# Fixed issue order from a table in place of ranks, in a packed-attention and gated-FFN kernel on one core

## The chip, the cores and the metric

The kernel runs on one core of a Trainium2 chip, in one launch. The metric is the device time of that launch in microseconds. Five instruction streams matter here: PE (matmuls and transposes), DVE, ACT, POOL and SP, which issues nearly all DMA transfers. Each stream runs in the order in which the program was written; an instruction that waits holds everything behind it on its own stream.

## What is computed

```python
def sm_attn(qq, kk, vv):                       # scale = 1/8
    a = softmax(scale * qq @ kk.T); return a @ vv
p_packed = sm_attn(p, k, v)                    # 32 queries per head over 576 rows
out      = sm_attn(q, p_packed, p_packed)      # 576 queries over 32 rows
x = out with the 8 heads side by side          # (8, 576, 512)
h = relu(x @ w_in)                             # (8, 576, 1024)
conv_out = 3-tap convolution of h along the sequence, per channel, with conv_w
return (h * sigmoid(conv_out)) @ w_out         # (8, 576, 512)
```

Batch 8, 8 heads, sequence 576, head dimension 64, float32 in and out.

## The kernel before, in words

The work is cut into streams, written as Python generators; each `yield Step(...)` says on which engine the next few instructions stand, what they wait for and which buffers they take and give back. There are 16 groups `g` of four heads (two groups a batch). For each group there is a stream for the loads of k, q (`load_kq`) and v (`load_v`), for the queries (`queries`: pm, pT), for the transposes of k and q (`head_transpose`: kT, qT; on PE and ACT for g < 4, one DVE transposition for g >= 4) and one for both attentions (`attention`: first scores from kT and pT, `nm`, exp into `a`, its transposes `a1T`, the product with v, `pb`, `ppT`, second scores from qT and ppT, softmax on DVE in tile `s`, transposed into `a2t`, split into `a2hi` on ACT and `a2lo` on DVE).

Weights come in eight transfers of 1 MB (`load_weight`), are decoded on ACT and DVE (tile `tmp`, L283 to L289) and put together on PE (`weight`, L341). For each batch `packed_weight` multiplies ppT into w_in, in two halves (`ghi`, `glo`). `ffn1(b, j)` makes one of 8 blocks of 128 channels of batch b: 12 matmuls (L649), relu into `hbuf` (L660), convolution on ACT and DVE (L664 to L670), sigmoid (L674), product (L676). `ffn2(m)` makes one of 36 tiles of 128 output rows: the split into `xhi` (ACT, L692) and `xlo` (DVE, L695), 24 matmuls into bank `fo` (L711), a copy into `o` (ACT, L716) and the output transfer (SP, L718).

Buffers bound how far streams run ahead: three `kq` slots for k and q of g >= 2, two slots for v, three PSUM tiles `big`, two for `s`, `x` and `o`. PE runs spare matmuls (`idle`, L259) where the planner saw a hole, up to the first output tile.

`Flow` is a planner that runs while the program is written. It holds a clock for each engine and for the transfers (`data`), and estimates for every step when it could start. `Flow.run` takes the engine that can go on first, and among the steps of that engine that are ready the one with the lowest rank in the table RANKS. So the ranks, with the costs in `Step`, set the order on every engine, and the SP queue's too. No estimate is left in the program that runs: only the order, and where the spare matmuls stand.

Of the kernel before, what the change touches and what calls it, by code (L numbers as in the profile page):

```python
# [20 lines left out]
RANKS = dict(  # L21
    k=[-411.0614, -56.32, -268.848, -369.0188, -10.607, 1.2892, 3.3386, 133.9183, 102.8098, 879.0292, 1255.3289, -152.1904, 3265.748, 2301.2373, 4073.7935, 5527.8193],
    v=[610.8614, 749.1152, 765.1742, 986.139, 1329.6858, 1269.6691, 1710.2848, 2149.7283, 1487.6843, 2549.2198, 5360.8956, 3717.5078, 5649.9351, 6699.0695, 6718.2568, 5821.5235],
    q=[153.3881, 2678.8613, -36.5409, -534.5143, 15.659, 555.9669, 1381.0816, 1482.4838, 1796.3623, 2083.4696, 3164.823, 3316.2358, 2551.7338, 5842.8484, 5523.9367, 5847.3967],
    queries=[5129.5747, -76.4517, 1831.777, 5486.9661, 2287.2198, 3228.3676, -560.937, 3911.8645, 5818.0089, 1224.2293, 2191.3475, 6075.1066, 4118.8338, 957.2377, -307.2209, 3615.5839],
    kT=[5736.7974, -483.8463, 553.7556, 408.255, 3083.2521, 5765.4763, 3896.7744, 5207.2595, 5358.4206, 3202.632, 5269.8891, 5371.5274, 5299.2063, 120.4482, 1271.3159, 2568.6227],
    qT=[1822.3814, 149.2968, 1218.3584, -269.2693, 1711.232, 1654.8561, 2171.3878, 3701.8394, 5672.096, 353.4709, 4066.7032, 5429.4678, 2268.9292, 5358.7206, 222.3705, 2101.3936],
    attention=[551.6318, 5443.0779, 4911.4625, 3277.6066, 65.8326, -4.185, 2216.4119, 775.0971, 3.0273, -63.566, 3554.4746, 194.6953, -141.7721, 2717.9598, 5675.3416, 2685.8275],
    sums=[2212.5273, 6593.67, 2120.4894, 2288.466, 2267.3881, 3298.9219, 539.0862, 5551.4175, 278.5043, 4140.9774, 2298.0652, 5441.9071, 5447.2342, 5340.7613, 2224.1344, 2195.0737],
    first=[3485.5317, 5992.9594],  # L30
    p=[-602.8021, 423.7176, 2583.1976, 2679.7272],
    load=[539.5951, 5201.6034, 3915.0356, -142.7698, -520.5537, 6101.7696, 3.6438, 3085.3699],
    weight=[3894.055, 415.5091, 5692.3927, 1094.9361, 2353.1416, 3840.1368, 5430.0718, 5676.1554],
    packed=[3577.1581, 5645.4193, 6697.6272, 2233.1226, 823.9014, 5464.0982, 4050.5266, 1240.3014, 1363.631, -311.5196, 5146.9566, 223.8075, 1458.215, 3320.7258, -22.7754, 5405.3068],
    ffn1=[382.8943, -307.4377, 670.6109, 3512.0211, 3061.8509, -696.3821, 708.7212, -523.2062, 2230.3122, 778.609, 3794.9833, 1385.1523, 171.9222, 5875.7606, 5891.3708, -268.9693, -27.916, 229.1412, 6086.4179, 3961.4117, 1253.6236, -298.9416, -92.0749, 506.8444, 1021.7865, 2235.1843, 1822.6814, 1818.6582, 289.8734, -373.3513, 123.6805, 971.6445, -505.8058, 2261.7916, 2059.7915, 2244.506, 2287.2636, 3251.6386, 4026.9332, 3882.595, 5829.3173, 1396.2015, 3883.7763, 6025.1134, -420.7776, 1005.7303, 426.1176, 4453.7934, 4265.8601, 1304.3038, 25.1843, -325.5138, 2534.8185, 47.5927, 5893.1673, 5388.9951, 5605.6557, 107.7366, 46.4049, 2226.8256, 5622.8384, 5211.2071, -79.5994, 387.443],
    ffn2=[3213.9683, 5587.2785, -45.6475, 2059.3311, 5970.2991, -826.7935, 1356.9098, 2161.583, -208.5721, 5444.3776, 960.4174, 2239.558, 966.066, 1050.7084, 5488.7732, 3774.109, 1199.7934, 5443.758, 5765.0603, 2151.9103, 5849.4642, 5597.3931, 4837.0348, -88.4009, 3979.5915, 2137.3678, 245.2455, 3761.219, 176.6706, 5898.133, 5524.2367, 204.1131, 1753.915, 261.0496, 165.4131, 5407.7056],
    hold=-10.7483,
# [14 lines left out]
class Flow:  # L52
# [32 lines left out]
    def add(self, rank, stream):
        step = next(stream, None)
        if step is not None:
            self.streams.append([rank, stream, step, (0.0, None)])

    def earliest(self, step, last):  # L90
        froms = [last]
        for event in step.after:
            if event not in self.done:
                return None
            froms.append(self.done[event])
        for name in set(step.take):
            n = step.take.count(name)
            if len(self.tokens[name]) < n:
                return None
            froms.append(self.tokens[name][n - 1])  # L100
# [49 lines left out]
    def run(self):  # L150
        while self.streams:
            ready = []
            for s in self.streams:
                at = self.earliest(s[2], s[3])
                if at is not None:
                    ready.append((at, s))
            assert ready, "no stream can go on"
# [1 line left out]
            engine = first[2].engine
            pick = None  # L160
            for at, s in ready:
                step = s[2]
                if step.engine != engine or at > now:
                    continue
# [1 line left out]
                if pick is None or rank < pick[0]:
                    pick = (rank, s)
            s = pick[1]
            step = s[2]
            at = now  # L170
# [23 lines left out]
            following = next(s[1], None)  # L194
            if following is None:
                self.streams.remove(s)
            else:
                s[2], s[3] = following, end
# [3 lines left out]
def tile_packed_attention_conv_gate(  # L202
# [517 lines left out]
    def add(kind, i, stream):  # L720
        flow.add(RANKS[kind][i], stream)

    for g in range(NGT):
        add("k", g, load_kq(g, "k", k))
        add("v", g, load_v(g))
        add("q", g, load_kq(g, "q", q))
        add("queries", g, queries(g))
        add("kT", g, head_transpose(g, "k"))
        add("qT", g, head_transpose(g, "q"))
        add("attention", g, attention(g))  # L730
        add("sums", g, sums(g))
    add("first", 0, conv_weight())
    add("first", 1, identities())
# [43 lines left out]
```

## Time and profile before

| | |
|---|---|
| time, median of three runs | 429.14 us (428.72 to 429.59) |
| the profiled execution: its own time, its span | 428.88 us, 426.9 us |
| PE busy, DVE busy, ACT busy in the span | 410.5 us (96%), 342.4 us (80%), 322.1 us (75%) |
| transfers | 47.2 MB, mean 111 GB/s over the span |

Span is from the first to the last instruction of the execution; the time has 1.98 us more around it. Matmuls are pipelined and their ends are modelled, so a busy PE is one that has work, not one at its peak. The busy share is a mean over stages: up to about 60 us the transfers move 218 to 357 GB/s in nearly every slice of the page, later 2 to 185.

### The profile page before, as it was taken

The page shows a single profiled execution, that of the slowest core. Times are in us where ns is not written, and L with a number is a line of the kernel's source. Part 1 is how long each engine was busy: PE and PEld are TensorE (multiplying, and loading weights), DVE is VectorE, ACT ScalarE, POOL GpSimd, SP SyncE. Part 2 cuts the span into 40 slices and gives each one's busy share as a digit, 9 for nine tenths or more (in the row PEclk, how much of TensorE's full clock was granted, in tenths as well). Part 3 has the DMA queues.
Part 4 walks back from the last instruction along what each step waited for, and adds up shares of the span by engine and source line. Part 5 has one row for each costly group of instructions (what it writes and reads, how often), then busy time and mean ns, then how long its engine had stood idle before and what let it go on. Part 6 is the DMA issues. An engine that isn't in the chain of part 4 may idle for free.

```text
span 426.9 us, 8189 instructions
## 1 busy us (share of the span) xinstructions
PE 410.5 (96%) x3347; PEld 325.6 (76%) x3347; DVE 342.4 (80%) x488; ACT 322.1 (75%) x509; POOL 1.6 (0%) x13
## 2 busy tenths in 40 slices
PE   4899989999999999999999999999999999999996
PEld 3665667777977797788778978877788888887885
DVE  0388889999998999999999798899889964865220
ACT  3697979999976978798876787889779865763221
POOL 1000000000000000000000000000000000000000
PEclk9999999999999999999999999999999999999999
DMA  8999998069478791782588039080110001000111
GB/s 298 357 272 345 218 254 140 2 85 175 77 141 166 97 185 44 150 122 81 83 150 122 26 95 146 2 137 26 40 36 26 25 25 51 25 26 25 51 49 49
DMA packets 135620, 47.21 MB, mean 111 GB/s; under 512 B 119700, under 2 KB 127892, under 8 KB 135584
## 3 DMA queue, kind: packets, MB, share of 16 engines
q1 hardware_dynamic: 135552, 46.67, 50.1%
q8 instruction: 26, 0.43, 0.5%
q14 instruction: 10, 0.08, 0.1%
q0 software_dynamic: 32, 0.02, 0.0%
HBM read 37.25 MB, written 9.44 MB: 109 GB/s over the span
## 4 chain that ended last, share of the span: by engine, by line
PE 83%; ACT 8%; DMA 5%; SPq 2%; DVE 1%; issue 1%; DVEq 0%; ACTq 0%
PE fo L711 42%; PE big L649 22%; PE sm L711 4%; PE big L460 3%; PE big L597 3%; PE sm L523 2%; PE big L514 2%; SPq L421 2%; DMA q<-in_q_dram 1%; DMA hgt<-in_k_dram 1%; PE big L341 1%; PE big L444 1%; DMA k<-in_k_dram 1%; PE idle L259 1%; DMA out_dram<-o 1%
## 5 line engine op out<-in xcount | busy, mean ns | idle before, releaser
L711 PE MATMUL fo<-wo_hi,xhi 128*128 128x512 f32 x264 | 106.7, 404 | 0.7 <-ACT o L716 0.7
L711 PE MATMUL fo<-wo_lo,xhi 128*128 128x512 f32 x264 | 104.4, 395 | 0.0
L711 PE MATMUL fo<-wo_hi,xlo 128*128 128x512 f32 x264 | 104.4, 395 | 0.0
L695 DVE TENSOR_TENSOR xlo<-hgt,xhi 128x1024 fp32r<-128x1024 f32 (+1 forms) x40 | 44.0, 1109 | 31.5 <-ACT xhi L692 28.6
L711 PEld LDWEIGHTS fo<-wo_hi,xhi 128*128 128x128 f32 x264 | 49.8, 188 | 14.4 <-ACT o L716 2.0
L711 PEld LDWEIGHTS fo<-wo_hi,xlo 128*128 128x128 f32 x264 | 49.6, 188 | 11.8
L711 PEld LDWEIGHTS fo<-wo_lo,xhi 128*128 128x128 f32 x264 | 49.8, 188 | 9.5
L649 PE MATMUL big<-a2hi,ghi 128*128 128x288 f32 x256 | 56.4, 301 | 0.6 <-DVE glo L620 0.4
L666 DVE SCALAR_TENSOR_TENSOR hgt<-hbuf,cw,hgt 128x576 f32<-128x576 f32 x64 | 51.6, 812 | 6.1 <-ACT hgt L664 5.6
L649 PE MATMUL big<-a2hi,glo 128*128 128x288 f32 x256 | 54.9, 295 | 0.0
L649 PE MATMUL big<-a2lo,ghi 128*128 128x288 f32 x256 | 54.8, 295 | 0.0
L676 DVE TENSOR_TENSOR hgt<-hgt,hbuf 128x576 f32<-128x576 f32 x64 | 47.4, 748 | 6.0 <-ACT hgt L674 6.0
L670 DVE SCALAR_TENSOR_TENSOR hgt<-hbuf,cw,hgt 128x576 f32<-128x576 f32 x64 | 51.5, 809 | 0.6
L674 ACT ACTIVATE hgt<-hgt 128x576 f32<-128x576 f32 x64 | 43.5, 685 | 10.6 <-DVE hgt L670 10.1
L692 ACT CAST xhi<-hgt 128x1024 fp32r<-128x1024 f32 (+1 forms) x40 | 38.2, 963 | 17.5 <-PE fo L711 15.8
L664 ACT ACTIVATE hgt<-hbuf,cw 128x576 f32<-128x576 f32 x64 | 49.6, 778 | 1.1
L660 ACT ACTIVATE hbuf<-big 128x576 f32<-128x576 f32 x64 | 41.3, 651 | 11.8 <-PE big L649 8.7
L649 PEld LDWEIGHTS big<-a2hi,ghi 128*128 128x128 f32 x256 | 42.0, 189 | 4.9 <-DVE s L547 0.8
L649 PEld LDWEIGHTS big<-a2lo,ghi 128*128 128x128 f32 x256 | 41.1, 188 | 0.0
L649 PEld LDWEIGHTS big<-a2hi,glo 128*128 128x128 f32 x256 | 41.0, 188 | 0.0
L716 ACT COPY o<-fo 128x512 f32<-128x512 f32 x33 | 19.2, 581 | 17.6 <-PE fo L711 13.6
L674 ACT ACT_TABLE_LOAD x15 | 19.2, 1283 | 0.3
(96 smaller groups left out, 565.8 us busy)
## 6 DMA issues: line engine op xcount, KB each, us to landing
out_dram<-o SPq DMA_DIRECT2D x36, 256.0 KB, 2.1
v<-in_v_dram SPq DMA_DIRECT2D x16, 512.0 KB, 5.8
k<-in_k_dram SPq DMA_DIRECT2D x48, 144.0 KB, 4.2
q<-in_q_dram SPq DMA_DIRECT2D x48, 144.0 KB, 4.1
hgt<-in_moe_w_in_dram SPq DMA_DIRECT2D x3, 1024.0 KB, 11.9
hgt<-in_moe_w_out_dram SPq DMA_DIRECT2D x3, 1024.0 KB, 10.4
q<-in_q_dram SPq DMA_DIRECT2D x2, 576.0 KB, 5.8
hgt<-in_k_dram SPq DMA_DIRECT2D x2, 576.0 KB, 7.5
```

The costliest lines, as they stand in the source:

```text
L460: nc.tensor.matmul(out=o.rearrange("c (j r) -> c j r", r=NR) if by_block(g) else o, lhsT=lhs[r, 32 * i : 32 * i + 32], rhs=rhs[r, :, h, :] ...
L649: nc.tensor.matmul(out=t[:, hf, :SH], lhsT=w[:, gg, js], rhs=x[:, hf * SH : (hf + 1) * SH], start=n == 0, stop=n == 3 * NG - 1,)
L660: nc.scalar.activation(out=h[:, 1 : S + 1].rearrange("c (f s) -> c f s", f=2), in_=t[:, :, :SH], func=AF.Relu)
L664: nc.scalar.activation(out=d, in_=h[:, 1 : S + 1], func=AF.Copy, scale=cw[:, NJ + j : NJ + j + 1])
L666: nc.vector.scalar_tensor_tensor(out=d, in0=h[:, 0:S], scalar=cw[:, j : j + 1], in1=d, op0=ALU.mult, op1=ALU.add)
L670: nc.vector.scalar_tensor_tensor(out=d, in0=h[:, 2 : S + 2], scalar=cw[:, 2 * NJ + j : 2 * NJ + j + 1], in1=d, op0=ALU.mult, op1=ALU.add)
L674: nc.scalar.activation(out=d, in_=d, func=AF.Sigmoid)
L676: nc.vector.tensor_tensor(out=d, in0=d, in1=h[:, 1 : S + 1], op=ALU.mult)
L692: nc.scalar.copy(out=hi[:, :, o], in_=src)
L695: nc.vector.tensor_tensor(out=lo[:, :, o], in0=src, in1=hi[:, :, o].bitcast(F32), op=ALU.subtract)
L711: nc.tensor.matmul(out=t, lhsT=x[:, c, :], rhs=w[:, c, :], start=c + i == 0, stop=c == NJ - 1 and i == 2)
L716: nc.scalar.copy(out=o, in_=t)
```

## The change

The ranks go. `ORDER` is a string of two-character numbers, 1525 in all; each names a stream by its place in the list of streams (k of group 0 is 00, v of group 0 is 01, and so on), and `Flow.run` takes the next step of that stream, whatever the planner's clock says. The planner's clocks now serve only to place the spare matmuls (29 of them in each program). The clock of the transfers starts at 4600 ns instead of 0. Three steps declare their buffers and their predecessors a little differently; this adds no instruction. Every instruction of the kernel before is there, apart from ACT's table loads, which are 26 instead of 30.

```diff
-RANKS = dict(
-    k=[-411.0614, -56.32, -268.848, -369.0188, -10.607, 1.2892, 3.3386, 133.9183, 102.8098, 879.0292, 1255.3289, -152.1904, 3265.748, 2301.2373, 4073.7935, 5527.8193],
...
+ORDER = (
+    "003k3m04020303040304080b0b04050b0j053k3l06060c0c0j0c0506013q0g06050j0c0e063r0o3u0k0k0r3k3k070e3k0e073k3r3r060906"
...
-        self.data = 0.0
+        self.data = 4600.0
...
-    def run(self):
...
-            now, first = min(ready, key=lambda x: x[0])
...
-                rank = s[0] + (RANKS["hold"] if step.table and self.table and step.table != self.table else 0.0)
...
+    def run(self, order):
+        for n in order:
+            s = self.streams[n]
+            step = s[1]
+            engine = step.engine
+            at = self.earliest(step, s[2])
...
-        yield Step("PE", 107, take=["sm"], give=["pb"], cols=256)
+        yield Step("PE", 107, take=["sm", "ppT"], give=["pb"], cols=256)
...
-        yield Step("ACT", 158, take=["ppT"], give=["sm"], sets=[("pp", g)])
+        yield Step("ACT", 158, give=["sm"], sets=[("pp", g)])
...
+        yield Step("PE", 556, after=[("qT", g)] + [("s2", g - 1)] * (g > 0), take=["big", "s2"], give=["qT"], sets=[("s2", g)], cols=1152, tiled=True)
...
-        yield Step("DVE", 669, take=["a2t"], give=["s2"])
+        yield Step("DVE", 669, after=[("hi", g - 1)] * (g > 0), take=["a2t"], give=["s2"])
...
-        flow.run()
+        flow.run([int(ORDER[i : i + 2], 36) for i in range(0, len(ORDER), 2)])
```

Where the instructions now stand is shown at three places. A line of the kernel before is 16 higher than the same line after the change.

**The start of SP's queue**, the first transfers of the program. Of before (q_91 is q of group 3, the first hgt0_76 row is k of group 0, k_98 and k_100 are k of groups 3 and 2):

```order
L477 DMA p_89<-in_p_dram 128x4x64
L410 DMA q_91<-in_q_dram 128x1152
L410 DMA hgt0_76<-in_k_dram 128x1152
L410 DMA k_98<-in_k_dram 128x1152
L410 DMA k_100<-in_k_dram 128x1152
L410 DMA hgt0_76<-in_k_dram 128x1152
L410 DMA hgt0_76<-in_q_dram 128x1152
```

And now (the rows of hgt0_76 are k of group 0, q of group 0, k of group 1):

```order
L394 DMA hgt0_76<-in_k_dram 128x1152
L461 DMA p_93<-in_p_dram 128x4x64
L394 DMA hgt0_76<-in_q_dram 128x1152
L394 DMA hgt0_76<-in_k_dram 128x1152
L378 DMA v_182<-in_v_dram 128x4x256
L382 DMA v_182<-in_v_dram 64x4x64
L296 DMA hgt1_77<-in_moe_w_in_dram 128x2x1024
L394 DMA k_186<-in_k_dram 128x1152
L394 DMA k_220<-in_k_dram 128x1152
```

The load of k of group 0 went from third to first, and q of group 3 left the front for a place far behind (second piece below).

**SP's queue further on**, from the load of q of group 1 on. Of before (k_316 is k of group 11, which DVE reads in its eighth kT transposition; q_400 is q of group 2):

```order
L410 DMA hgt0_76<-in_q_dram 128x1152
L312 DMA hgt1_77<-in_moe_w_in_dram 128x2x1024
L394 DMA v_267<-in_v_dram 128x4x256
L398 DMA v_267<-in_v_dram 64x4x64
L421 DMA k_316<-in_k_dram 32x36x32 x4
L312 DMA hgt1_77<-in_moe_w_in_dram 128x2x1024
L410 DMA q_400<-in_q_dram 128x1152
L394 DMA v_409<-in_v_dram 128x4x256
```

And now (k_631 is k of group 4, q_385 and q_388 are q of groups 2 and 3):

```order
L296 DMA hgt1_77<-in_moe_w_in_dram 128x2x1024
L394 DMA q_385<-in_q_dram 128x1152
L394 DMA q_388<-in_q_dram 128x1152
L378 DMA v_419<-in_v_dram 128x4x256
L382 DMA v_419<-in_v_dram 64x4x64
L296 DMA stage_70<-in_moe_w_out_dram 128x2x1024
L296 DMA hgt1_77<-in_moe_w_out_dram 128x2x1024
L378 DMA v_586<-in_v_dram 128x4x256
L382 DMA v_586<-in_v_dram 64x4x64
L405 DMA k_631<-in_k_dram 32x36x32 x4
L296 DMA hgt1_77<-in_moe_w_out_dram 128x2x1024
```

The four transfers of group 11's k no longer stand ahead of the last w_in tile, of q and of the w_out tiles; the first k loaded in this form is that of group 4, behind two tiles of w_out.

**Around the first block of ffn1**, on DVE first. Of before (kT<-k is group 4's transposition, a2lo group 1's last piece, wo_lo a weight's decoding):

```order
L553 TENSOR_TENSOR s_661<-s_661,mx 128x576
L289 SCALAR_TENSOR_TENSOR wo_lo<-hgt_77,tmp 128x1024
L433 STREAM_TRANSPOSE kT<-k 128x1152
L560 TENSOR_REDUCE sm_714<-s_661 128x18
L577 TENSOR_TENSOR a2lo<-a2t,a2hi 128x576
L547 STREAM_TRANSPOSE s_745<-big 128x576
L503 TENSOR_REDUCE nm<-big 128x1
```

And now:

```order
L537 TENSOR_TENSOR s_601<-s_601,mx 128x576
L561 TENSOR_TENSOR a2lo<-a2t,a2hi 128x576
L273 SCALAR_TENSOR_TENSOR wo_lo<-hgt_77,tmp 128x1024
L417 STREAM_TRANSPOSE kT<-k 128x1152
L544 TENSOR_REDUCE sm_675<-s_601 128x18
L531 STREAM_TRANSPOSE s_710<-big 128x576
L546 TENSOR_SCALAR sm_675<-sm_675 128x18
```

The a2lo of group 1 went from behind the kT transposition and a sum to ahead of both and of a weight's decoding.

PE at the same place. Of before (qT,ppT is group 3's second score, kT,pT group 4's first score, big<-a2hi,ghi the first matmuls of ffn1):

```order
L613 MATMUL big<-ghi,minus 128x512 x2
L259 MATMUL idle<-ident 128x128 x3
L460 MATMUL big<-qT,ppT 32x288 x8
L460 MATMUL big<-kT,pT 32x288 x8
L487 MATMUL sm<-ident,pm 128x128
L259 MATMUL idle<-ident 128x128
L649 MATMUL big<-a2hi,ghi 128x288 x2
L649 MATMUL big<-a2lo,ghi 128x288 x2
```

And now:

```order
L597 MATMUL big<-ghi,minus 128x512 x2
L523 MATMUL sm<-ident,pb 128x128
L243 MATMUL idle<-ident 128x128 x3
L444 MATMUL big<-qT,ppT 32x288 x8
L633 MATMUL big<-a2hi,ghi 128x288 x2
L633 MATMUL big<-a2lo,ghi 128x288 x2
L633 MATMUL big<-a2hi,glo 128x288 x2
L633 MATMUL big<-a2hi,ghi 128x288 x2
L633 MATMUL big<-a2lo,ghi 128x288 x2
L633 MATMUL big<-a2hi,glo 128x288 x2
L444 MATMUL big<-kT,pT 32x288 x8
```

The first score of group 4 and a query transpose stood ahead of ffn1's first block; the score now stands behind it.

## Rows read from the trace of the kernel before

**Rows 1.** Stretches: length; PE, PEld, DVE, ACT, POOL busy; granted clock; DMA share; GB/s.
```profile
91.88:424.00 332.12, 330.18 (x2560) 269.04 (x2558) 273.52 (x380) 246.97 (x381) 0.00 (x0) 1.00 0.42 79
10.00:20.00 10.00, 8.60 (x113) 6.50 (x113) 2.97 (x6) 5.80 (x13) 0.00 (x0) 1.00 1.07 357
18.00:55.15 37.15, 33.80 (x413) 20.90 (x413) 30.25 (x48) 32.41 (x58) 0.00 (x0) 1.00 1.03 289
60.00:69.00 9.00, 8.97 (x89) 7.15 (x88) 8.82 (x17) 8.94 (x15) 0.00 (x0) 1.00 1.11 130
100.00:120.00 20.00, 19.78 (x174) 16.98 (x167) 19.96 (x30) 17.00 (x29) 0.00 (x0) 1.00 0.59 108
```

**Rows 2.** PE in order of time: start, length, instruction, idle before and its releaser.
```profile
8.05 1.33 PE L444 MATMUL big<-ident,hgt 128*128 128x128 f32 x5 [0.29 <-DMA hgt<-in_k_dram]
...
56.06 0.72 PE L460 MATMUL big<-kT,pT 64*32 64x288 f32 x16 [1.86 <-DVE kT L433]
...
57.02 0.52 PE L649 MATMUL big<-a2hi,ghi 128*128 128x288 f32 x2
...
91.88 0.48 PE L711 MATMUL fo<-wo_hi,xhi 128*128 128x512 f32 x1
...
132.18 0.50 PE L711 MATMUL fo<-wo_hi,xhi 128*128 128x512 f32 x1
...
137.09 0.53 PE L649 MATMUL big<-a2hi,ghi 128*128 128x288 f32 x2 [0.38 <-DVE glo L620]
```

**Rows 3.** ACT in order of time, 36 to 90 us.
```profile
36.69 1.13 ACT L283 ACTIVATE tmp<-hgt 128x1024 f32<-128x1024 f32 x1 [1.14 <-DMA hgt<-in_moe_w_in_dram]
...
45.90 0.73 ACT L575 CAST a2hi<-a2t 128x576 fp32r<-128x576 f32 x1
46.96 1.18 ACT L283 ACTIVATE tmp<-hgt 128x1024 f32<-128x1024 f32 x1 [0.33 <-DMA hgt<-in_moe_w_out_dram]
...
57.08 0.27 ACT L495 COPY pT<-sm 128x128 f32<-128x128 f32 x1 [1.79 <-PE sm L487]
58.02 1.16 ACT L283 ACTIVATE tmp<-hgt 128x1024 f32<-128x1024 f32 x1 [0.68 <-DMA hgt<-in_moe_w_out_dram]
...
67.52 0.35 ACT L534 ACTIVATE pb<-sm,rs 128x128 f32<-128x128 f32 x1
...
89.31 1.07 ACT L692 CAST xhi<-hgt 128x1024 fp32r<-128x1024 f32 x1
```

**Rows 4.** DVE in order of time, 54 to 172 us.
```profile
54.53 1.38 DVE L433 STREAM_TRANSPOSE kT<-k 128x1152 f32<-128x1152 f32 x1 [2.50 <-DMA k<-in_k_dram]
...
56.47 0.74 DVE L577 TENSOR_TENSOR a2lo<-a2t,a2hi 128x576 fp32r<-128x576 f32 x1
...
90.76 1.23 DVE L695 TENSOR_TENSOR xlo<-hgt,xhi 128x1024 fp32r<-128x1024 f32 x1
...
130.10 1.29 DVE L695 TENSOR_TENSOR xlo<-hgt,xhi 128x512 fp32r<-128x512 f32 x2
...
171.75 1.38 DVE L433 STREAM_TRANSPOSE kT<-k 128x1152 f32<-128x1152 f32 x1
```

**Rows 5.** SP's queue in order of time: issue start, time at the queue's head.
```profile
0.74 0.43 SPq L477 DMA_DIRECT2D p<-in_p_dram  x1
1.24 0.49 SPq L410 DMA_DIRECT2D q<-in_q_dram  x1
1.78 0.42 SPq L410 DMA_DIRECT2D hgt<-in_k_dram  x1
...
22.59 8.13 SPq L421 DMA_DIRECT2D k<-in_k_dram  x4
...
54.33 14.73 SPq L421 DMA_DIRECT2D k<-in_k_dram  x8
```

**Rows 6.** DMA issues of 0 to 12 us: count, KB each, us to landing.
```profile
q<-in_q_dram SPq DMA_DIRECT2D x1, 576.0 KB, 5.3
```

**Rows 7.** Waits of SP's queue, longest in total: us in all, times, longest.
```profile
SPq L421 <- DVE kT L433: 36.7, 6, 16.8
```

More of the change, by code (lines that the diff above doesn't have):

```diff
@@ L16 @@
 PSUM = bass.MemoryType.PSUM
-RANKS = dict(
-    k=[-411.0614, -56.32, -268.848, -369.0188, -10.607, 1.2892, 3.3386, 133.9183, 102.8098, 879.0292, 1255.3289, -152.1904, 3265.748, 2301.2373, 4073.7935, 5527.8193],
[L23 to L37, printed above, removed]
@@ new lines @@
+ORDER = (
+    "003k3m04020303040304080b0b04050b0j053k3l06060c0c0j0c0506013q0g06050j0c0e063r0o3u0k0k0r3k3k070e3k0e073k3r3r060906"
+    "0k0k0e0f0f3r06060e0m0m3k3k0a06063v3v0r0r3s060s0s3v0e3n0s0m0d3w0i060q3v0e0e0m0s0d0d0e060606060n0h40060d3r3t3t3t0z"
+    "0z0m3r0u0u0u0z3x0e3t0n3v3v170e06063t3t0l0l3x0e0m0m3x3y0e0e3x0e0v0e060e0e46460u0u0l0m4641410e410v413x0l0m0p46170m"
+    "0m3x3z3z0m170t3z47410w0m0u0e0e423z10471f0t0u0m0m41410t0t470u0u0u0u3z47480m0u0m120u434848121249490u490m144843480u"
+    "49434a4a123z4849484a4a490u494a0u444b12453z43454a4a0m4b150x4c4c1f1f4g4c4c124d4b4b43434g4g4c0u4b4d4c4c4d4d4b4b0m0m"
+    "4d434g4e4e4d0u0u454d4f4f0u454h4h4h4f4f4e4e454h4f4f4i4i4e4e45184i1a4f4e1c4i1313456e6e4j4j124j0y1a4k4k4k4i4j4k1212"
+    "164i4i6e6e4k6f1a6e6e6e6e6e4k6e1n1g1a1a114l6e4l4l6f4j121i4k1i1b1b1a124j4j4l1212191i4m4m1a4m1j4m4m6f4n1a4n3o1l1a6g"
+    "6f6f1n6f6f1a4q4n1n124m4l4l6g1a4m4l4n1j121a1d1s1k6f6f6f1v6f6f4o4o1o4n4p4o4o4o124p4p4q204p4p6h4q6h4o6g1i1i6g1v6g6g"
+    "1v1a6g6g6g6g4n236g6g12124p4n121q1i1i4r4p1q4o23231a1q1w126i1a1a6i1a121a1a6h6h6h6h6h6h1q1q6h6h4r6h1t1e6h6e1y1y6j1a"
+    "1a1r1r1q1q1y246i6i6i6i6i1h4r4s4s4s4s4t4t2b1m1y6i4t1z4s2b2b291z4t4t6i1y1i1i284s4t2626261y1i1i4u4u6i6i6i4s6j4t4v1y"
+    "4v4u4v1p1i1i4v1u3p212j4u4u2c4w2g6k6k1q6j6j6j266j6j6j6j6j4w1q1i4w4w1i1i4u6j262e274u2e4w4w501q1q4v1i4w4v2j2j6k2o6k"
+    "6k6k6k2e6l4v2k1q1q6l1y6k4x4x501y6k6k6k6k4y2a271i1i4y4y1x4y4y4z4z1q1q226l6l1y1y262r4z6m6m264x4x4x6l2e2e2r6l6l6l1i"
+    "1i1q1q4z4z4x4x1q6l6l512m2r6l4y4z4z4y1q1q6n51501q6m6m6m6l6j6m6m6m6m6m6m6m2h2f26526n6n1y2m2f516n6o52521y2m1y535354"
+    "5426546n256n6n6n6o5252521y5454541y52262e2w6n6n5326546p6n555555262d261y26531y5a536o2m566o6o6o26556p55262z2e2e5353"
+    "36561y5a556o556o565626566o6o6o5a2e6o6q56566q265757576p1y6p2z6p5758582s582p596p1y59596p6p6p6p572m2657266p2z585858"
+    "572n5959595b2e2u2u582m592e262n6q2i6q6q6q6q2u6q2u6q6q6p2x6r6r2e2m375b6q6q2e2e5c5b2l305c5c5c6r375d2e6s5d5d5e6r5e5c"
+    "2q2v5d5d375c5e5c5e5d2u5d6r6r6r5e5e2e5e3f6r6r6r2m2m5f5f5f5g5g6s5h2v2m2u325f2e5f2e5g5g2m345g6t6r6r5h6t5f5f6s6s5g5h"
+    "6s2u2m5h5h2e6s6s6s6s5g6s6s6s5i5i6t6t5h2e5i2m385i6t6t2m6u6t6t2u2u6t6t322m2m2m2t6u5i5j2m326t5j3f5k5k5j6n6t2e5h5l5l"
+    "6v5i2m2m6v335k326u6u6u2m6u6u6u6u6u6u5i5j5j5m5m5j5l5m3f5j326v6v5n5n5n5m3c5m5m5n5n5o5o2y6v5m332u32325o5n3a3a3g3a6v"
+    "5p5p6v6v6v326v5n5o5o6w6w316v5o5q5q3a2u5o3b6w6w6v6u356w6w5r5q3a5p5q32325p5p2u2u3b5q5r6x5r5r5p5p3i5u5q5u3a326w6w6w"
+    "6w6w6w6x5r5q395s5s3i325r2u2u2u6y2u6y6x6x6x6x6x6x6x5s6x3i3a3j3j6x6z5t5t5t5s2u5r5s32322u32326y6y6y6y3i6y6y6y6z6y5s"
+    "2u3i6y323e3a3a5v3d5v2u5s5t5t5t5u3i3a6z5t6x7032323270326z6z6z6z6z6z6z6z3i5v5w5w5w6z5w5w5x5x5x5x5x5y5y705y3a5y3i3i"
+    "705w5x5x71703h5y5w3a717070707070705z6y70605y5z5z5y5z726060713i3i5z5z6064643i3i3a5z7261617171717171613a3a3i717171"
+    "717362623a3a3a6160603a613i3i3a723a6072737272727272727263626363636161643i7474633i73737373737373737373653i3i746262"
+    "74636274747474637474743i6275666674726667676775686666666667677575756975756565687668687575756867676868766975756969"
+    "6a6a6a6b7676696a6a6b6969766a6b6b6b6b6a76767676766c77776c76766d78786c6d6d7777777777777777776b6d6d6d6c6c6c6c6d7779"
+    "797878787878787878787979797a7a79797979797a79797b7b7a7a7a787a7a7a7a7a7a7b7b7b7c7c7b7b7b7b7b7b7b7c7c7c7c7c7d7d7c7c"
+    "7c7c7c7d7d7d7d7d7d7d7d7d7d"
@@ L83, in __init__, with add @@
         self.streams = []
[L85 to L88, printed above, removed]
+    def add(self, stream):
+        self.streams.append([stream, next(stream), (0.0, None)])
     def earliest(self, step, last):
         froms = [last]
[L92 to L100, printed above, removed]
+        froms += [self.done[event] for event in step.after]
+        froms += [self.tokens[name][step.take.count(name) - 1] for name in step.take]
         at = max(t + self.LAG[e][step.engine] if e else 0.0 for t, e in froms)
@@ L148, in transfers @@
         return at, self.data
-    def run(self):
[L151 to L157, printed above, removed]
-            now, first = min(ready, key=lambda x: x[0])
[L159 to L164, printed above, removed]
-                rank = s[0] + (RANKS["hold"] if step.table and self.table and step.table != self.table else 0.0)
[L166 to L170, printed above, removed]
+    def run(self, order):
[4 more added lines that the diff above has]
+            at = self.earliest(step, s[2])
             if step.table is not None:
@@ L193, in run @@
                 self.done[event] = end
[L194 to L198, printed above, removed]
+            s[1:] = next(s[0], None), end
 @with_exitstack
@@ L568, in attention @@
         )
-        yield Step("DVE", 669, take=["a2t"], give=["s2"])
+        yield Step("DVE", 669, after=[("hi", g - 1)] * (g > 0), take=["a2t"], give=["s2"])
         at = wk.tile([128, S], F32, name="a2t", tag="a2t", bufs=1)
         nc.vector.transpose(out=at, in_=s2)
-        yield Step("ACT", 573, after=[("hi", g - 1)] * (g > 0), take=["a2"], sets=[("hi", g)])
+        yield Step("ACT", 573, take=["a2"], sets=[("hi", g)])
         hi = wk.tile([128, S], F32R, name="a2hi", tag="a2hi", bufs=4)
@@ L718, in ffn2 @@
         nc.sync.dma_start(out=out.rearrange("b s f -> (b s) f")[m * 128 : (m + 1) * 128, :], in_=o)
-    def add(kind, i, stream):
-        flow.add(RANKS[kind][i], stream)
     for g in range(NGT):
[L724 to L733, printed above, removed]
+        flow.add(load_kq(g, "k", k))
+        flow.add(load_v(g))
+        flow.add(load_kq(g, "q", q))
+        flow.add(queries(g))
+        flow.add(head_transpose(g, "k"))
+        flow.add(head_transpose(g, "q"))
+        flow.add(attention(g))
+        flow.add(sums(g))
+    flow.add(conv_weight())
+    flow.add(identities())
     for i in range(NGT // 4):
-        add("p", i, load_p(i))
+        flow.add(load_p(i))
     for i in range(8):
-        add("load", i, load_weight(i))
-        add("weight", i, weight(i))
+        flow.add(load_weight(i))
+        flow.add(weight(i))
     for b in range(B):
         for hf in range(2):
-            add("packed", 2 * b + hf, packed_weight(b, hf))
+            flow.add(packed_weight(b, hf))
         for j in range(NJ):
-            add("ffn1", NJ * b + j, ffn1(b, j))
+            flow.add(ffn1(b, j))
     for m in range(NTT):
-        add("ffn2", m, ffn2(m))
+        flow.add(ffn2(m))
     with tc.manual_schedule():
-        flow.run()
+        flow.run([int(ORDER[i : i + 2], 36) for i in range(0, len(ORDER), 2)])
 _INS = ["q", "k", "v", "p", "moe_w_in", "moe_conv_w", "moe_w_out"]
```

1 line of the change is left out of this document (removed).

## The prediction

> **What bounds the kernel now.** I read busy time by stretch first, cut at the first matmul of the first output tile, 91.88 us [rows 2]. Behind that point, up to 424 us, PE is busy 330.2 of 332.1 us [rows 1]. So the last 332 us are PE's own work, and an order can win at most 1.9 us there. What an order can change is when PE gets to 91.88.
>
> Then I read the three engines in order of time for what ends the waits ahead of that point. PE's first real work starts at 8.05, when k of group 0 lands [rows 2]. From 18 to 55 us the transfers run full (DMA share 1.03, 289 GB/s), ACT is busy 32.4 of 37.2 us and DVE 30.3 [rows 1]. ACT waits there for weights, 1.14 us at 36.69 and 0.33 at 46.96, and again 0.68 at 58.02 [rows 3]. Between lies one knot. DVE waits 2.50 us for k of group 4 and starts its transposition at 54.53 [rows 4]; PE waits 1.86 us for that at 56.06 [rows 2]; ACT waits 1.79 us for a small PE transpose queued behind that score, until 57.08 [rows 3]. Group 1's a2lo, which ffn1 needs, stands on DVE behind the transposition and runs at 56.47 [rows 4], although its a2hi was made at 45.90 [rows 3]. PE's first block of ffn1 starts at 57.02 [rows 2]. From then on ACT and DVE have no gap worth the name (8.94 and 8.82 of 9.00 us from 60 to 69 [rows 1]) until the xhi at 89.31 [rows 3] and the xlo at 90.76 [rows 4] release the first output tile. So a microsecond won on ACT and DVE ahead of 57 us arrives at 91.88, and from there at the end.
>
> **The change part by part.**
>
> *First transfers.* k of group 0 is issued third, at 1.78 [rows 5], and PE can start 6.27 us later, at 8.05. It is now issued first, in the place at 0.74. With its own 6.27 us it would be there at 7.01, a gain of 1.0. The transfer of the same size that stood in front of it, q of group 3, landed 5.3 us after its issue [rows 6]; with that, k is there at 6.04, a gain of 2.0. If also the bytes go that stood ahead of it (590 KB of q and 131 KB of p, 2.0 us at the 357 GB/s of 10 to 20 us [rows 1]), it takes 4.25 us, is there at 4.99, and the gain is 3.1. I take 2.0: q of group 3 is the nearest row, with one small transfer ahead of it. The five spare matmuls that now stand ahead of the first transposes run while PE waits. p is now second; its short chain (pm, pT) runs beside the transposes of k and their copies. If that cover were gone it would cost the 1.65 us that 590 KB take at 357 GB/s. The Trainium skill (DMA: Bandwidth & Descriptors, Queues, rings and completion order) says that each DMA engine takes descriptors of one issuing queue in ring order. By that rule what is issued behind k cannot hold it, the gain would be the 3.1 us, and the sum below would end 1.1 us lower. The trace doesn't settle it.
>
> *The load of group 11's k.* Before, four transfers of k for group 11 hold the head of SP's queue for 8.13 us from 22.59 on [rows 5]. DVE reads them at 171.75 [rows 4]. In the new order they leave the front. Two such loads, eight issues, hold the queue for 14.73 us from 54.33 on [rows 5]; from 60 to 69 us they move 130 GB/s at a DMA share of 1.11 [rows 1], so one of 590 KB fills the DMA engines for about 4.5 us, against 1.65 us by its bytes at 357 GB/s. Everything behind it, the last w_in tile, q, and the w_out tiles, can land up to 4.5 us earlier, and v of group 3 and a load of p no longer stand ahead of the w_out tiles either. ACT will ask for these weights earlier too, by 2 to 5 us. Of the three waits for weights, 2.15 us in sum, I take half: 1.1, bounds 0 and 2.15.
>
> *The knot at 52 to 57 us.* Group 1's a2lo now stands ahead of the kT transposition, and ffn1's first block ahead of group 4's score. DVE had run out of work at 52.03 (54.53 less 2.50), so a2lo can run 4.4 us earlier than 56.47 even if nothing else moves. Group 4's k is still behind two w_out tiles and may be late again; then DVE waits for it with ffn1's matmuls already under way, and PE has work. I take ACT's 1.79 us as gone. The other end is nothing, if ACT finds the next wait at once.
>
> *ACT's work ahead of the first xhi.* Counted in the two orders, it is the same but for pb and ppT of group 4, which move behind it. The pb is 0.35 us [rows 3]; I count that and nothing for ppT. DVE has two instructions fewer ahead of the first xlo, which I count at nothing, since ACT carries the stretch.
>
> *New waits.* Of ACT's 4.74 us without work from 18 to 55 us [rows 1], 1.47 are the two waits for weights; 3.27 us are short waits for PE and DVE. Another order has others. Bounds: none more, and as much again, 3.3. I take a quarter, 0.8.
>
> *Table loads.* ACT has four fewer, but none of them ahead of the first xhi. Behind 91.88 ACT is busy 247 of 332 us [rows 1]: nothing.
>
> *Behind the first output tile.* DVE is the one to watch. From 100 to 120 us it is busy 19.96 of 20 us [rows 1]. The xlo of tile 4, started at 130.10 and 1.29 long [rows 4], is done 0.8 us ahead of PE at 132.18 [rows 2]. Up to that xlo DVE has in the new order one a2lo, one normalising product and three short instructions fewer than before, so the cover is no thinner. Nothing counted; it is the second rival below.
>
> Sum: 2.0 + 1.1 + 1.79 + 0.35 - 0.8 = 4.4 us. The profiled execution took 428.88 us, with 1.98 us around its span of 426.9. 428.9 - 4.4 = 424.5. The median before, 429.14, is 0.26 above that execution, so the median to expect is **424.7 us**. Own range, with the terms at their ends but not all at once: gains from 2.3 (1.0 + 1.79 + 0.35 - 0.8) to 7.3 (3.1 + 2.15 + 1.79 + 0.35), that is 421.8 to 426.8.
>
> **The rivals.** 0.2%, about what a measurement of this kernel can tell from no change, is 0.86 us.
>
> *The transfers pace the front.* For it: the DMA share of 1.03 from 18 to 55 us. The load of group 11's k may cost no more than its bytes, 1.65 us, and the waits on weights only move. Then the front follows the transfers and gains those 1.65 us: 427.5. Against it: 130 GB/s at a full share, and the knot, where an order and not a rate made ffn1 wait. The Trainium skill (DMA: Bandwidth & Descriptors, Where 436 GB/s comes from) puts the HBM limit of one core at about 358 GB/s for such loads. By that rule the front cannot move bytes faster whatever their order, which speaks for this rival. The trace's best stretch, 357 GB/s, agrees.
>
> *The gain is lost between 92 and 137 us: no change.* DVE is full there and 0.8 us ahead of PE; at 137.09 PE already waits 0.38 us for a glo on DVE [rows 2]. To bring the gain under 0.86 us, PE must lose some 3.6 us there. Two waits on DVE like that at 54.53, 2.50 us each less the 0.8 of cover, would do: 428.3 to 430.0. Against it: DVE's list up to tile 4 is no longer than before.
>
> *An output transfer caught behind a load: slower.* In the new order loads of k and q for groups 6 to 9 stand on SP around the first output transfers. Such loads wait for a slot that a transposition on DVE frees, 16.8 us at the longest now [rows 7]. Behind a caught output stand the two `o` slots, then ACT's copy, bank `fo` and PE. The slots cover two tiles; tiles 0 to 4 start 10.1 us apart on the mean (91.88 to 132.18), so 20 us. Beyond that each microsecond is PE's; from 24.6 us of waiting on it is slower than before. At 27 us: 7 - 4.4 = 2.6 us over, 431.7. For it: loads now come to these slots in another mix. Against it: the slot that group 11's k held until 171.75 is free for them.
>
> **How the numbers follow.** Forecast 0.70, the transfers as bound 0.10, given back 0.09, slower 0.07, more than the forecast's range holds 0.04. Faster by over 0.2%: 0.70 + 0.10 + 0.04 = 0.84; within: 0.09; slower: 0.07. The range is to leave out no more than 0.2: 421.5 cuts off the 0.04, 428.4 the last two rivals, 0.16.
>
> **What the changed profile would show.** PE's first transposes at about 6.0 instead of 8.05. No issue of 8 us on SP ahead of 30 us. The first block of ffn1 at 52 to 54 us, with no wait on kT ahead of it. The first output tile at about 87.5. PE busy in the rest to within 2 us of its length. The forecast is wrong if the first tile starts at 87.5 but PE has holes behind it (second or third rival), if the first tile is past 90 us with ACT waiting for weights (first), or if PE starts no earlier than 7 us.

## The result, and the profile after

The changed kernel ran at 422.49 us (median of six, 421.15 to 424.02), the kernel before beside it at 428.93. The ratio is 0.9854, interval 0.9828 to 0.988: faster by 6.4 us (6.3 by the ratio), where 4.4 were forecast. The profiled execution took 422.01 us, its span is 420.2.

The page, busy time of the changed kernel:

```profile
PE 410.4 (98%) x3347; PEld 324.4 (77%) x3347; DVE 343.6 (82%) x488; ACT 316.3 (75%) x505; POOL 1.6 (0%) x13
```

Stretches of the changed kernel (columns as in [rows 1]): up to its first xhi, from its first output tile on, a stretch of fast transfers, and three stretches that were cut for before:

```profile
0.00:81.73 81.73, 76.31 (x767) 53.92 (x768) 64.52 (x104) 71.42 (x124) 1.58 (x13) 0.98 0.86 238
84.49:417.00 332.51, 331.36 (x2561) 267.68 (x2559) 276.44 (x381) 242.23 (x379) 0.00 (x0) 1.00 0.44 81
...
14.00:18.00 4.00, 4.00 (x73) 3.16 (x70) 1.24 (x5) 3.42 (x6) 0.00 (x0) 1.00 1.02 408
...
18.00:55.15 37.15, 36.50 (x424) 23.38 (x417) 35.85 (x60) 35.30 (x65) 0.00 (x0) 1.00 1.03 290
60.00:69.00 9.00, 8.71 (x98) 6.37 (x97) 8.97 (x15) 9.00 (x14) 0.00 (x0) 1.00 1.15 152
100.00:120.00 20.00, 20.00 (x188) 14.73 (x187) 19.38 (x28) 16.12 (x29) 0.00 (x0) 1.00 0.86 130
```

From 18 to 55 us the transfers move as many bytes as before (290 GB/s against 289 [rows 1]) at the same share, but ACT works 35.3 us there instead of 32.4 and DVE 35.9 instead of 30.3. Over the whole stretch the order moved no more bytes, but it put other bytes first and moved more of them early: from 26 to 34 us 372 GB/s, against 187 before (rows with e1 below).

PE, ACT, DVE and SP's queue of the changed kernel in order of time:

```profile
0.74 0.38 SPq L394 DMA_DIRECT2D hgt<-in_k_dram  x1
...
4.82 1.18 PE L428 MATMUL big<-ident,hgt 128*128 128x128 f32 x5
...
8.92 1.11 PE L428 MATMUL big<-ident,hgt 128*128 128x128 f32 x5 [1.43 <-DMA hgt<-in_q_dram]
9.96 1.21 PE L444 MATMUL big<-kT,pT 64*32 64x288 f32 x16
...
30.95 0.74 ACT L491 ACTIVATE a<-big,nm 128x576 f32<-128x576 f32 x1 [0.95 <-DVE nm L487]
...
33.68 9.52 SPq L405 DMA_DIRECT2D k<-in_k_dram  x4
...
44.23 7.27 SPq L405 DMA_DIRECT2D k<-in_k_dram  x4
...
46.15 0.76 DVE L561 TENSOR_TENSOR a2lo<-a2t,a2hi 128x576 fp32r<-128x576 f32 x1
...
47.96 1.38 DVE L417 STREAM_TRANSPOSE kT<-k 128x1152 f32<-128x1152 f32 x1
...
49.86 0.53 PE L633 MATMUL big<-a2hi,ghi 128*128 128x288 f32 x2
...
81.73 1.05 ACT L676 CAST xhi<-hgt 128x1024 fp32r<-128x1024 f32 x1
...
82.81 1.23 DVE L679 TENSOR_TENSOR xlo<-hgt,xhi 128x1024 fp32r<-128x1024 f32 x1
...
83.07 0.66 ACT L644 ACTIVATE hbuf<-big 128x576 f32<-128x576 f32 x1 [0.29 <-PE big L633]
...
84.49 0.48 PE L695 MATMUL fo<-wo_hi,xhi 128*128 128x512 f32 x1
```

The reader is to see five things. The first transposes start 3.2 us earlier than in [rows 2], but the first score only 1.9 earlier (in the trace of before it starts at 11.86), since q's transposes ahead of it wait 1.43 us. The view lists no wait of ACT between 30.95 and 83.07; the four waits of [rows 3] are gone. The first issues of 7 to 10 us on SP come at 33.68 and 44.23, not at 22.59 as in [rows 5]. Group 4's kT runs at 47.96 instead of 54.53 [rows 4] with no wait. And the lead over [rows 2] is 7.2 us at the first ffn1 block, 7.4 at the first output tile; at PE's last matmul (it starts at 422.94 before and at 416.16 after) it is 6.8. PE did not idle behind the first tile (1.15 us of 332.51). Its busy time there is 1.2 us longer than in [rows 1]; by the two orders only one query transpose, about 0.3 us, moved behind the tile.

A ledger of ACT up to the first xhi says where the 7.6 us came from. In the kernel before:

```profile
0.00:89.31 89.31, 77.75 (x769) 53.99 (x770) 66.27 (x106) 72.57 (x127) 1.58 (x13) 1.00 0.83 227
```

ACT is busy 72.57 us and idle 16.74 before, busy 71.42 and idle 10.31 after: 6.4 us less idling and 1.15 us less work ahead of the xhi. A part of that work is the decoding of weights: the "float32 in" of the opening holds for q, k, v and p, while the weights come as 64-bit numbers (a transfer of 1 MB is 256 by 512 of them).

### The profile page after: what moved, and what is told of

The parts are those of the page before. It is cut to its first block, busy times and chain, and to the rows that moved or that the text cites. A ratio compares the mean times of both kernels' runs of the same rounds, so it can differ in the third digit from the quotient of the medians.

```text
span 420.2 us, 8196 instructions
## 1 busy us (share of the span) xinstructions
PE 410.4 (98%) x3347; PEld 324.4 (77%) x3347; DVE 343.6 (82%) x488; ACT 316.3 (75%) x505; POOL 1.6 (0%) x13
## 4 chain that ended last, share of the span: by engine, by line
PE 85%; ACT 4%; DVE 1%; issue 0%; ACTq 0%
PE fo L695 45%; PE big L633 23%; PE sm L695 4%; PE big L444 4%; PE big L581 3%; PE sm L507 2%; PE big L498 2%; PE big L325 1%; ACT hgt L658 0%; ACT wo_lo L329 0%; ACT hbuf L644 0%; PE sm L523 0%; PE idle L243 0%; PE sm L471 0%; ACT L658 0%
## 5 line engine op out<-in xcount | busy, mean ns | idle before, releaser
L695 PE MATMUL fo<-wo_hi,xhi 128*128 128x512 f32 x264 | 107.6, 408 | 0.7 <-ACT o L700 0.7
L487 DVE TENSOR_REDUCE nm<-big 128x1 f32<-128x576 f32 x16 | 12.0, 749 | 14.9 <-PE big L444 14.8
```

Source lines behind the costliest of these rows:

```text
L695: nc.tensor.matmul(out=t, lhsT=x[:, c, :], rhs=w[:, c, :], start=c + i == 0, stop=c == NJ - 1 and i == 2)
```

## The experiments

All kernels compute everything. Those on the order of before have that order written out as a table, with the old clock of 0; with nothing else changed this gives the instruction stream of before on every engine. Differences in microseconds are ratios times 429. Single profiled executions lie up to 1.2 us off their median, so sizes are taken from the ratios, and mechanisms from the traces.

**e1_k11_later**: only group 11's k load moved.

```diff
 queries 3, sums 1
-load k 11                 (entry 74)
 kT 2, attention 1, queries 4
...
 load k 10                 (entry 489)
+load k 11
```

> The order of before, with one entry moved: the load of group 11's k goes from behind the first k loads to behind group 10's k load, so that the 8 us that it holds the SP queue ahead of 30 us are free for the weights' pieces and group 4's k. Theory (the prediction's): the waits of ScalarE for weight pieces and of VectorE for group 4's k go with it, 1.1 to 4 us, 425 to 428 us. Rival (the loads pace the front by their bytes alone, so the waits only move): at most the bytes of one k load, 1.65 us, or nothing: 427.3 to 429. The landing of group 4's k tells them apart: well ahead of 50 us by the theory, still above 52 by the rival.

Measured 425.84 us, ratio 0.9939 (0.9921 to 0.9958): 2.6 us gained, 1.8 to 3.4. Its DVE and PE in order of time, and the stretch up to its first xhi:

```profile
51.48 1.37 DVE L417 STREAM_TRANSPOSE kT<-k 128x1152 f32<-128x1152 f32 x1
...
54.46 0.54 PE L633 MATMUL big<-a2hi,ghi 128*128 128x288 f32 x2 [0.18 <-ACT glo L601]
```

```profile
0.00:85.76 85.76, 76.57 (x765) 53.46 (x766) 65.58 (x106) 72.05 (x127) 1.59 (x13) 1.00 0.84 237
```

Group 4's k is there before DVE comes for it, all four waits of ACT in [rows 3] are gone, and ACT idles 3.0 us less (85.76 less 72.05 is 13.71, against 16.74). When that k landed can't be read, as nothing waits for it; more than its 1.65 us of bytes was won. The transfers from 26 to 34 us show why (of before, of e1, of the changed kernel):

```profile
26.00:34.00 8.00, 7.76 (x47) 4.56 (x46) 7.66 (x15) 6.96 (x16) 0.00 (x0) 1.00 1.00 187
...
26.00:34.00 8.00, 7.74 (x50) 4.58 (x48) 7.32 (x14) 6.89 (x14) 0.00 (x0) 1.00 1.09 347
...
26.00:34.00 8.00, 8.00 (x57) 4.19 (x56) 7.30 (x15) 7.05 (x15) 0.00 (x0) 1.00 1.05 372
```

The DMA engines are full in all three, but with group 11's k among the transfers they move about half as much. The 1.28 MB that before moves less than e1 in these 8 us would take 3.7 us at e1's 347 GB/s (an estimate).

**e12_k11_behind_k4**: the same load, but only 20 us later.

```diff
-load k 11                 (entry 74)
...
 load k 4                  (entry 157)
+load k 11
```

> The order of before, with group 11's k load behind group 4's k load, some 20 us later than before, but still far too early: it keeps one of the three buffers of k and q, as before, and takes the queue for about 8 us there. Theory (the 8 us on the queue ahead of the weights' pieces and of group 4's k were the price): most of the gain of the kernel with that load behind group 10's stays, 425.5 to 427 us. Rival (the price was the buffer held for over 100 us, so that later k and q loads wait for two others): no gain, 428.3 us or more.

426.80 us, ratio 0.9956 (0.9936 to 0.9976): 1.9 us of the 2.6, although the buffer is held for only some 20 us less. So what the load takes ahead of the weights and of group 4's k, on the queue and on the DMA engines (no run tells these two apart), was most of the price, not the buffer. The interval overlaps e1's, so whether the buffer costs anything is open. In its trace one weight comes late again: ACT waits 1.99 us for a w_out piece at 57.00.

**e2_k0_first**: only the first transfers.

```diff
+load k 0
 load p 0
-load q 3
-load k 0
 ...
 load k 2 ... load q 2
+load q 3
```

> The order of before, with two entries moved: group 0's k is loaded first, and group 3's q, which was the second load, goes behind group 2's k and q. Theory: the first transposes start near 5 us instead of 8.05 and the first score up to 2 us earlier; passed on, that is 1 to 2 us, 427 to 428 us. Rival: the next wait (group 11's long load and the weights behind it) takes it back, so the first ffn1 block starts at 57 us as before and the time is 428.5 to 429.3.

429.16 us, ratio 1.0016 (0.9999 to 1.0033): nothing. Its start, ACT and PE:

```profile
6.69 0.31 ACT L267 ACTIVATE s<-s 24x128 f32<-24x128 f32 x1 [0.72 <-DMA s<-in_moe_conv_w_dram]
6.91 0.29 ACT L468 ACTIVATE pm<-p 128x128 f32<-128x128 f32 x1
...
7.25 0.48 PE L471 MATMUL sm<-ident,pm 128*128 128x128 f32 x1 [0.74 <-ACT pm L468]
7.52 1.27 PE L428 MATMUL big<-ident,hgt 128*128 128x128 f32 x5
```

k was there (e16 below, with the same first transfers, starts its transposes at 5.22), but in e2 they stand on PE behind the second queries' transpose. That needs a pm on ACT, which stands behind the conv weights, and those land at 6.69 from POOL's own transfer. The first transposes moved by 0.5 us, and the theory fell: an early load needs an early place in the work. In the trace the 0.5 us are still there at the first xhi (88.77 against 89.31); the times do not show them.

**e3_both** and **e16_front_chain**: both loads moved; in the second also the first chain of work.

```diff
 load k 0, load p 0, ..., queries 0 (pm, transpose, pT)
+kT 0 (PE, ACT, PE, ACT), score of group 0
 conv weights (ACT), queries 1, conv weights (DVE, PE, ACT) ...
-kT 0 ... score of group 0
```

> The order of before with both loads moved: group 11's k behind group 10's, and group 0's k first with group 3's q behind group 2's. Theory (the 0.5 us that the first score gained alone was lost again at the late weights' pieces, which are gone now): 0.5 us or more below the kernel with group 11's load alone, 425.3 us or less. Rival (without a new order of the work the first loads give nothing, since the first transposes stand behind the conv weights' steps): within 0.5 us of it, 425.3 to 426.4 us.

> The same two loads moved, and in the work of the engines one chain: group 0's k transposes, their copies and the first score stand directly behind the first queries, ahead of the conv weights' steps and of the second queries. Theory (first transfers and the order of the first work are one term, about 2 us): first transposes below 6.5 us, first score 2 us earlier or more, and 1 to 2.5 us below the kernel with group 11's load alone, 423.3 to 424.8 us. Rival (the front is bound behind, by v and q that land later, so the lead of the first score is not passed on): 425.3 us or more.

e3: 425.63 us, ratio 0.9925 (0.9907 to 0.9943), the rival: 0.6 us past e1 with the intervals largely over each other. e16: 424.20 us, ratio 0.9898 (0.9875 to 0.9921), 1.8 us past e1, the intervals just touching. Its PE:

```profile
5.22 1.27 PE L428 MATMUL big<-ident,hgt 128*128 128x128 f32 x5
...
8.88 0.84 PE L444 MATMUL big<-kT,pT 64*32 64x288 f32 x16 [0.25 <-ACT kT L434]
```

The first score is 3.0 us earlier than before, by the theory. Of that some 1.8 is passed on by the ratio. Its profiled execution (425.34 us, 1.1 above the median) does not show it: there the first ffn1 block starts at 54.29, 0.2 us ahead of e1's, and the first xhi at 85.60, as in e3. So that it is passed on rests on the times alone, and these fall into two groups, 424.05 to 424.20 and 425.34 to 425.39.

**e4_knot**: only the places at 52 to 57 us.

```diff
 DVE
+a2lo of group 1
 kT 4
-a2lo of group 1
 PE
+first block of ffn1
 score of group 4
 queries 6 (transpose)
-first block of ffn1
```

> The order of before, with three entries moved at 52 to 57 us only: on VectorE the low half of group 1's weights goes ahead of the transpose of group 4's k, for which VectorE waits 2.5 us; on TensorE the first ffn1 block goes ahead of group 4's score. The loads stay. Theory (the knot is a price of its own, 1.8 us): first ffn1 block near 55 us, 427.0 to 427.4 us. Rival (the knot is only where the late load shows, and the next wait for it takes the gain): first ffn1 near 55 but the first output tile within 0.5 us of before, 428.4 to 429.3 us.

429.02 us, ratio 1.0009 (0.9998 to 1.0021): the rival. Its DVE, PE and ACT:

```profile
53.02 0.75 DVE L561 TENSOR_TENSOR a2lo<-a2t,a2hi 128x576 fp32r<-128x576 f32 x1
...
54.79 0.53 PE L633 MATMUL big<-a2hi,ghi 128*128 128x288 f32 x2
...
57.62 0.27 ACT L479 COPY pT<-sm 128x128 f32<-128x128 f32 x1 [1.67 <-PE sm L471]
```

ffn1 comes 2.2 us earlier, but ACT's wait for the queries' transpose stays at 1.67 us (1.79 in [rows 3]), because the score and that transpose still stand behind the late k. The first xhi starts at 89.06, 0.25 us earlier. What counted in the knot was ACT's wait, and only an earlier k took it away (e1). That transpose can't go ahead of the score: it takes the buffer that the score gives back.

**e10_loads_of_after**: all of SP's transfers in the changed order, all other work in the order of before.

```diff
-SP: order of before
+SP: order of after
 PE, ACT, DVE: order of before
```

> The transfers on the SP queue in the order of the changed kernel, all of them, and the work of TensorE, ScalarE and VectorE in the order of before. Theory (the order of the loads is the change): at least 4 of the 6.4 us, 422.5 to 425 us. Rival (the order of the work carries it, the loads only allow it): 427 to 429 us, or more, since before's order of work was made for other landings. Between 425 and 427 both share it.

434.99 us, ratio 1.0146 (1.0126 to 1.0166): slower than before: the rival, and further than its figures. Three of its waits, on ACT, DVE and PE, with the start of its first output tile between them, and the stretch from that tile on:

```profile
27.34 0.31 ACT L468 ACTIVATE pm<-p 128x128 f32<-128x128 f32 x1 [5.04 <-DMA p<-in_p_dram]
...
91.08 0.48 PE L695 MATMUL fo<-wo_hi,xhi 128*128 128x512 f32 x1
...
113.16 1.38 DVE L417 STREAM_TRANSPOSE kT<-k 128x1152 f32<-128x1152 f32 x1 [3.66 <-DMA k<-in_k_dram]
...
122.90 0.72 PE L444 MATMUL big<-qT,ppT 64*32 64x288 f32 x16 [3.17 <-DVE qT L417]
```

```profile
91.08:428.50 337.42, 331.96 (x2560) 269.80 (x2558) 273.79 (x380) 246.84 (x380) 0.00 (x0) 0.99 0.43 80
```

The second p was put behind weights by an order whose ACT asks for it later. Even so the first output tile starts 0.8 us earlier than in [rows 2]. The loss lies behind it: a k comes late to DVE at 113.16, PE waits 3.17 us for DVE at 122.90 and is without work for 5.5 of 337.42 us in all, and its last matmul starts at 428.10, 5.2 us later than before. That is the way of the prediction's second rival. PE is full behind the first tile only as long as the order brings the later loads in time. The order of the transfers is worth nothing without the order of the work.

**e13_start_of_after** and **e14_start_of_before**: the two orders spliced.

```diff
-ORDER = the changed table
+e13: its first 153 entries, then what is left in e1's order
+e14: the first 88 entries of e1's order, then what is left in the changed order
```

> The first 153 steps of the changed order (up to some 40 us), then the steps that are left in the order of before with group 11's k load behind group 10's; the clock at 4600. The kernel that moves that load alone ran at 425.8 us, the changed one at 422.5. Theory (the rest of the gain is made in the first 40 us): 422 to 423.8 us. Rival (it is made behind, in the order of the first ffn1 blocks and the output tiles): 425 to 427 us. In between, both.

> The other way round: the first 88 steps of the order of before (up to some 24 us) without group 11's k load, then the steps that are left in the changed order; the clock at 0. Theory (the rest of the gain is made in the first 24 to 40 us): 424.5 to 426.5 us, near the kernel that moves the one load alone. Rival (it is made behind): 422 to 423.5 us.

e13: 424.23 us, ratio 0.9892 (0.9862 to 0.9922). e14: 424.37 us, ratio 0.9898 (0.9871 to 0.9925). Both come out between the theories. By the times the new start gives 2.0 us past e1, the new order behind it 1.8, each with an interval that only touches or barely overlaps e1's. The stretch from 24 to 40 us has the new order in both, so these two figures may count the same gain twice. From e14 to the changed kernel, which differ in the start and in the planner's clock alone, it is 1.9 us by the ratios (2.3 to e7 below, which has e14's clock), again with overlapping intervals. Up to its first xhi e14 reads:

```profile
0.00:83.72 83.72, 75.86 (x757) 53.14 (x758) 65.11 (x104) 71.45 (x124) 1.58 (x13) 1.00 0.86 232
```

ACT idles 12.27 us and works 71.45, against 13.71 and 72.05 in e1: the order between 24 us and the first output tile wins on both sides, 1.4 and 0.6 us. In it the short waits of ACT that e1 still has between 39 and 51 us (0.20, 0.26 and 0.37) are gone. The first xhi starts at 89.31 before, at 85.76 in e1, at 83.72 in e14 and at 81.73 in the changed kernel: steps of 3.6, 2.0 and 2.0 us. The trace of e13 does not show its gain (425.26 us, the slowest of its six executions):

```profile
85.56 1.07 ACT L676 CAST xhi<-hgt 128x1024 fp32r<-128x1024 f32 x1
```

That is 0.2 us ahead of e1. As in e16, that the new start is passed on when the order of before follows it rests on the times alone; in traces it is seen only with the new order behind it.

**e7_clock_0, e9_score_first, e18_score_first_clock_0**: the changed order with the planner's clock at 0 (e7), with the first score ahead of group 0's q transposes (e9), with both (e18).

```diff
-        self.data = 4600.0
+        self.data = 0.0
...
+score of group 0
 qT 0 (PE, ACT)
-score of group 0
```

> The changed kernel's order, with the planner's transfer clock back at its old start of 0. The clock only decides where spare matmuls are put on TensorE. Theory (the order alone is the change): 422 to 423 us, within 0.2% of the changed kernel. Rival (the shifted clock matters, since a spare matmul put into a wait that is not there delays TensorE): 423.5 us or more.

> The changed kernel with one entry moved: the first score goes ahead of group 0's q transposes, which wait 1.43 us for their load at 8.92 us. Theory (the wait stands in the way of the first softmax and so of the rest): first score near 8 us, 421 to 422 us. Rival (the second step of group 0 needs q anyway, so the lead is lost there): 422.2 to 422.9 us.

> The same move with the planner's clock at 0, the best of the versions if both hold: 420.5 to 421.6 us by the theory that the wait counts, 421.7 to 422.5 by its rival.

e7: 421.99 us, ratio 0.9844 (0.9814 to 0.9873), not to be told from the changed kernel: the order alone is the change. e9: 423.05 us, ratio 0.9865 (0.9843 to 0.9887), nearer the rival, by which the lead of the first score is not passed on. e18: 421.11 us, ratio 0.9821 (0.9801 to 0.9842), in the theory's range, below e9 on the same chip with intervals that do not meet, and the fastest kernel here; against the changed kernel the intervals overlap. So the move of the score costs 0.5 us with the one clock (e9 against the changed kernel) and gains 1.0 with the other (e18 against e7), both within overlapping intervals: what the wait for q is worth stays open. PE of e9, then of e18:

```profile
2.52 2.50 PE L243 MATMUL idle<-ident 128*128 128x128 f32 x10 [2.52 <-POOL ident masks.py:199]
4.81 1.27 PE L428 MATMUL big<-ident,hgt 128*128 128x128 f32 x5
...
7.95 0.72 PE L444 MATMUL big<-kT,pT 64*32 64x288 f32 x16
```

```profile
4.49 1.30 PE L428 MATMUL big<-ident,hgt 128*128 128x128 f32 x5 [4.49 <-DMA hgt<-in_k_dram]
...
7.96 1.22 PE L444 MATMUL big<-kT,pT 64*32 64x288 f32 x16
```

With the shifted clock the planner believes that the first load lands later, and puts ten spare matmuls ahead of the first transposes, which then wait 0.3 us for them. That the clock is worth the whole 1.9 us between e9 and e18 is not shown: e7 and the changed kernel differ by the same clock and by 0.4 us. The clock's shift did not make the change fast; whether it costs is open.

## Why the prediction was right, and where its sizes were off

The mechanism holds: PE is full behind the first output tile, so what is won on ACT and DVE ahead of it arrives at the end (7.6 us at the first xhi, 6.4 in the times). The sum, 4.4, is 2 us short, and two of the signs that it named were missed: the first ffn1 block came at 49.86, not at 52 to 54, and the first output tile at 84.49, not at 87.5. By the steps:

- *First transfers*, 2.0 with bounds of 1.0 to 3.1. PE could start 3.2 us earlier, the far bound: 4.25 us were worked out from issue to start, and it is 4.1 (0.74 to 4.82), or 3.7 in e18, where no spare matmuls stand ahead. The page named there (the Trainium skill, DMA: Bandwidth & Descriptors, Queues, rings and completion order) states that each DMA engine takes descriptors in ring order. The 4.1 us fit that; that nothing issued behind k holds it is not isolated by any run. But the step took the landing for the start of the work. Alone it gave nothing (e2). With the chain of work moved too, and with group 11's load out of the way, 1.8 us came through by the times (e16), and from e14 to the changed kernel 1.9. So the size came out by luck, for a reason that the step didn't have.
- *The load of group 11's k*, 1.1, and *the knot*, 1.79: 2.9 in sum, measured 2.6 for that one load (e1). They were one term: the knot is where the late k shows, and its own edit gave nothing (e4). All of ACT's waits for weights went, not half.
- *ACT's work ahead of the first xhi*, 0.35: it is 1.15 us. By the two orders three instructions moved behind it: the pb that was counted, the ppT (0.27 us) that was put at nothing, and a pm (0.32) that the count had missed.
- *New waits*, a loss of 0.8: none is seen; ACT's idling ahead of the xhi fell by 6.4 us in all. This is the term with the wrong sign. It asked only what the new order could spoil between 18 and 55 us, and e14 shows that the order from 24 us on takes 1.4 us of ACT's idling away.
- *Behind the first output tile*: 0.6 us of the lead goes, not to a wait but to 1.2 us more of PE's busy time. One query transpose is some 0.3 of that; the 264 matmuls fo<-wo_hi,xhi behind it read 107.6 us in sum instead of 106.7, and the cause of that is open.

So 2.6 (one load, before to e1), about 1.8 (the order from 24 us on, e1 to e14) and about 1.9 (the start, e14 to the changed kernel) make the 6.3 us of the ratio. Each of the last two is known to about 1.5 us. Why the rivals fell: "the transfers pace the front" allowed 1.65 us, ACT's work from 18 to 55 us rose with the bytes unchanged, and from 26 to 34 us the same full DMA engines move 187 GB/s in the one order and 372 in the other; "the gain is lost between 92 and 137 us" would need holes on PE, as e10 has them, and here PE is busy 331.36 of 332.51 us; the output transfers wait on their own copies, and loads into the slots that kT frees wait 12.8 us at the longest (16.8 in [rows 7]). Waits of SP's queue in the changed kernel:

```profile
SPq L702 <- ACT o L700: 175.3, 25, 16.3
...
SPq L405 <- DVE kT L417: 17.6, 2, 12.8
```

## What to carry to other kernels

When one stage is full and the ramp ahead of it is not, look on the load queue for one transfer that is early without need and slow for its bytes; moving that one entry gave 40% of what the whole table gave. A load that lands earlier is worth nothing until the instruction that reads it is first in its engine's queue, and an order of transfers taken without its order of work can cost more than it wins, and lose it behind the ramp, where the full engine then waits. A wait that shows at three engines at once has one price, so count it at the engine that paces the stretch.
